# Deeper fetching of expert block rows, gating sums in four column groups, and paced weight transfers

## The chip, the cores and the metric

The kernel runs on one core of a Trainium2 chip. The metric is the device time of one execution in microseconds (us); the median of several runs is compared. A core has a matrix engine (TensorE, written PE in the profile, with its weight loads as PEld), a vector engine (VectorE, DVE), a scalar engine (ScalarE, ACT), a general engine (GpSimd, POOL) and a queue engine (SyncE, SP) that here issues most transfers. Each engine works through its own instructions in order; semaphores order them against each other and against the DMA transfers.

## The reference

Sliding-window attention with ALiBi bias, then a mixture of experts with a dense layer beside it. Shapes: q, k, v are 8 batches x 8 heads x 576 positions x 64; x has 4608 rows of 512; 8 experts, each 512 x 512 twice.

```python
scores = scale * np.matmul(q, k.transpose(0, 1, 3, 2))
mask = (rel >= 0) & (rel < 128)
scores = np.where(mask, scores + bias[None], -1000000000.0)
attn = softmax(scores)
attn_out = np.matmul(attn, v)
x = attn_out.transpose(0, 2, 1, 3).reshape(B * S, H * D)

y_dense = np.maximum(x @ w1_dense, 0.0) @ w2_dense
logits = x @ w_gate
expert_idx = np.argmax(logits, axis=1)
gate_w = softmax(logits)[np.arange(N), expert_idx]
for e in range(E):
    mask = expert_idx == e
    h = np.maximum(x[mask] @ w1[e], 0.0)
    y_moe[mask] = gate_w[mask, None] * (h @ w2[e])
return y_dense + y_moe
```

## The kernel before

**Attention.** The work is cut into 16 units (`u`): a batch and one half of its heads (four heads). A unit has three steps (`pr`): key blocks 0 and 1, 2 and 3, and the last of 64 rows; 48 steps in all. The main loop at L966 counts `n`. In round `n` it computes the scores of step `n` (`scores`, L353: a mask matmul L371, score matmuls L382, an exponential on ACT L392, and later a DVE subtraction L411 for the low half of the probabilities), multiplies the probabilities of step `n-1` with v (`attend`, L445), divides by the row sums on DVE (`norm`, L460 to L467, whose result is the tile `xf`), and transposes step `n-3` (`flip`, L488) into `xT` (fp32, for the gating) and `xTb` (bf16, for the dense layer). Rows of q, k and v of the next units are fetched by SP (`load_q` L153, `load_k` L141, `load_v` L167). `kraw` and `qraw` have one buffer each, so a fetch waits until DVE has turned the unit before (`turn`, L175). Unit 2's q is asked for twice, once ahead of the loop (L961) and once in round 1 (L1016); the second transfer follows the first.

**Gating.** When a unit's last step has been transposed, `gate_a` multiplies its half of x with its rows of `w_gate`. It runs for each half of the 576 columns: two fp32 matmuls into two 32-partition groups of a PSUM tile (L510) and one ACT copy into the tile `lt`, named `ltsb` in the profile (L517). The first half runs ahead of `attend`, the second behind it. After a batch's second unit, `gate_b` adds the groups: five fp32 matmuls with the selector `sel` (L525). An fp32 matmul is two instructions in the profile. `gate_bv`, `gate_c` and `gate_d` find the expert, the slot within the expert's rows and the gate weight, and POOL scatters the rows of x into `xs_dram` (L599). `dense1` (L647, L654) and `dense2` (L662, L670) compute the dense layer, and POOL scatters it into `ys_dram` at the same slots (L671). The small PSUM tiles of `flip`, gating and dense layer share two buffers of one tag (`misc`). The tile `yt` behind L671 has four buffers.

**Weights.** The 18 weight matrices go into `w_all` with a cast from fp32 to bf16, on POOL's queue (`load_weights`, L89). The loop sends the next one when its index is at most `2 + 16 (n-3) / 42`, which puts the first three in rounds 0, 1 and 3. From round 5 on, each is preceded by `pace` (L690): a one-element copy on POOL from `xf` into the destination, so that the transfer waits for the attention to get that far.

**Expert blocks.** Once six batches are routed, 16 blocks of 128 rows, all of one expert each, can be placed (`route_early`); the other 27 follow after the last batch (`route_late`), where SP also writes 8 pairs of fill rows behind each expert's last row (L826, L830). The blocks start in round 50, together with the last batch's dense layer, one block a round; from block 8 on they are alone. `fetch(j)` (L838) loads the block's first row into a register of SP and issues two transfers: `xr` (rows of x with gate weight and token number) and `yr` (the dense result), from four buffers each. Blocks 16 on wait for all rows and fills. `block(j)` does, in this order on PE: `turn_h(j)` (four transposes, L900, copied by ACT L904), `layer1(j+1)` (four matmuls L885, ACT L893), `turn_x(j+2)` (four transposes L864, copied by DVE L870), `layer2(j)` (four matmuls L912), then DVE adds `yr` (L920) and POOL scatters the sum to the output (L921), reading the token numbers out of `xr`. So a buffer of `xr` is free when its scatter has read it to the end. Last comes `fetch(j + AHEAD + 1)`; `AHEAD` is 3.

The order of instructions on PE, ACT and DVE is that of the program text; POOL's and SP's are set by the scheduler. SP and POOL spread their transfers over eight semaphores each, and a transfer waits until the one that had its semaphore before it is done.

Of the kernel before, what the change touches and what calls it, by code (L numbers as in the profile page):

```python
# [9 lines left out]
F32 = mybir.dt.float32  # L10
F32R = mybir.dt.float32r
BF16 = mybir.dt.bfloat16
I32 = mybir.dt.int32

ALU = mybir.AluOpType
ACT = mybir.ActivationFunctionType
AX = mybir.AxisListType
# [6 lines left out]
def kernel(  # L24
# [12 lines left out]
    nc = tc.nc  # L37

    B, H, S, D = q.shape
    E = moe_w_gate.shape[1]  # L40
    FF = moe_w1_dense.shape[1]
    DM = H * D
    NTOK = B * S
    P = 128
# [4 lines left out]
    NT = (S + P - 1) // P  # L49
    SP_ = NT * P  # L50
    HQ = H // 4
    NU = B * HQ
    R = S // 32
    PW = 2 * P
# [3 lines left out]
    NB = NTOK // P + E - 1  # L58
# [9 lines left out]
    RW = XW + 4  # L68
# [4 lines left out]
    consts = ctx.enter_context(tc.tile_pool(name="consts", bufs=1))  # L73
# [21 lines left out]
    dbuf = ph0.enter_context(tc.tile_pool(name="dbuf", bufs=1))  # L95
# [30 lines left out]
    for i in range(2):  # L126
        xrow = dbuf.tile([P, NT, RW], F32, name=f"xrow{i}")
        nc.gpsimd.memset(xrow[:, :, TC + 1 : RW], 0.0)
        xrows.append(xrow)
    lt = dbuf.tile([P, SP_], F32, name="ltsb")  # L130
    nc.gpsimd.memset(lt[:, S:SP_], 0.0)

    raw = {}
    tmp = {}
# [78 lines left out]

    mask = consts.tile([P, H, 2 * PW], BF16, name="mask")

    sc = [ppool.tile([P, 2, 2 * PW], F32, name="p32", tag=f"p32_{2 * PW}") for _ in range(2)]
    d_i, d_f = sc[0].bitcast(I32)[:, 0, :], sc[0][:, 1, :]
    inv, big = sc[1][:, 0, :], sc[1][:, 1, :]
    nc.gpsimd.iota(
# [38 lines left out]
    def more_constants():  # L258
        for h in range(4, H):
            mask_head(h)  # L260
        ut_f = ident_x["ut_f"]
        nc.vector.tensor_copy(out=ut_b, in_=ut_f)
        nc.vector.memset(ones_b, 1.0)
        nc.vector.tensor_reduce(
            out=sel,
            in_=ident_f.rearrange("p (c x) -> p x c", c=4)[:, 0:E, :],
            op=ALU.add,
            axis=AX.X,
        )
        nc.vector.tensor_single_scalar(  # L270
            out=m_div, in_=pidx_i, scalar=5, op=ALU.logical_shift_right
        )
        nc.vector.tensor_single_scalar(
            out=m_mod, in_=pidx_i, scalar=31, op=ALU.bitwise_and
        )
        nc.vector.tensor_copy(out=m_divf, in_=m_div)
        nc.vector.tensor_copy(out=m_modf, in_=m_mod)
        for i in range(NT):
            nc.vector.scalar_tensor_tensor(
                out=tok_c[:, i : i + 1],  # L280
                in0=m_modf,
                scalar=4.0 if i < NT - 1 else 2.0,
                in1=m_divf,
                op0=ALU.mult,
                op1=ALU.add,
            )
            nc.vector.tensor_scalar_add(
                out=tok_c[:, i : i + 1], in0=tok_c[:, i : i + 1], scalar1=float(i * P)
            )
        nc.vector.tensor_copy(out=em8, in_=em8_i)  # L290
        nc.vector.memset(em8[TAIL:P, NT - 1, :], 0.0)
        nc.vector.tensor_copy(out=em8x, in_=em8)
        nc.vector.memset(em8x[TAIL:P, NT - 1, :], 1.0)
        for i in range(2):
            nc.vector.memset(ohs[i][:, NT, :], 0.0)
        nc.vector.tensor_copy(out=base0, in_=base_i)
        nc.vector.tensor_copy(out=basee, in_=base_i)
        nc.vector.tensor_copy(out=jf, in_=jf_i)
        nc.vector.memset(fill_x, 0.0)
        nc.vector.tensor_copy(out=fill_x.bitcast(I32)[:, TC : TC + 1], in_=oob_f)  # L300

    ut_b = consts.tile([P, P], BF16, name="ut_b")
    ones_b = consts.tile([P, P], BF16, name="ones_b")
    sel = consts.tile([P, E], F32, name="sel")
    m_div = consts.tile([P, 1], I32, name="m_div")
    m_mod = consts.tile([P, 1], I32, name="m_mod")
    m_divf = consts.tile([P, 1], F32, name="m_divf")
# [12 lines left out]
    ident_x = {}  # L320

    def pool_constants():
        ut_f = ppool.tile([P, 2, 2 * PW], F32, name="p32", tag=f"p32_{2 * PW}")[:, 0, 0:P]
        nc.gpsimd.memset(ut_f, 1.0)
        nc.gpsimd.affine_select(
            out=ut_f,
            in_=ut_f,
            compare_op=ALU.is_gt,
            fill=0.0,
            base=0,  # L330
            pattern=[[1, P]],
            channel_multiplier=-1,
        )
        ident_x["ut_f"] = ut_f
        nc.gpsimd.memset(wg_pad, 0.0)
        nc.sync.dma_start(
            out=wg_pad[:, :, 0:E], in_=moe_w_gate.rearrange("(ds p) e -> p ds e", p=P)
        )
        nc.gpsimd.iota(em8_i, pattern=[[0, NT], [1, E]], base=-E, channel_multiplier=0)
        nc.gpsimd.iota(base_i, pattern=[[ST, E]], base=0, channel_multiplier=0)  # L340
        nc.gpsimd.iota(jf_i, pattern=[[1, NB]], base=0, channel_multiplier=0)

    wg_pad = consts.tile([P, 4, 32], F32, name="wg_pad")
    em8_i = consts.tile([P, NT, E], I32, name="em8_i")
    base_i = consts.tile([P, E], I32, name="base_i")
    jf_i = consts.tile([P, NB], I32, name="jf_i")
    pool_constants()


# [70 lines left out]
    cur = {}  # L420
# [80 lines left out]

    gst = {}

    def gate_a(u, hf):
        h0 = 64 * (u % HQ)
        HF = S // 2
        lp = psum_m.tile([P, 512], F32, name="lp", tag="misc")
        for c in range(2):
            r0 = h0 + 32 * c
            nc.tensor.matmul(  # L510
                out=lp[r0 : r0 + 32, 0:HF],
                lhsT=wg_pad[:, 2 * (u % HQ) + c, :],
                rhs=cur["xT"][:, c, hf * HF : (hf + 1) * HF],
                start=True,
                stop=True,
            )
        nc.scalar.copy(  # L517
            out=lt[h0 : h0 + 64, hf * HF : (hf + 1) * HF],
            in_=lp[h0 : h0 + 64, 0:HF],
        )  # L520

    def gate_b(b):
        gst["lg"] = lg = psum_m.tile([P, NT, E], F32, name="lg", tag="misc")
        for t in range(NT):
            nc.tensor.matmul(  # L525
                out=lg[:, t, :],
                lhsT=lt[:, t * P : (t + 1) * P],
                rhs=sel,
                start=True,
                stop=True,  # L530
            )

    def gate_bv(b):
        lg = gst["lg"]
# [86 lines left out]
    def after(nm, ins, nb):  # L621

        for b, name in writers[nm]:
            if b < nb:
# [5 lines left out]
                    ),  # L630
                    reason="rows written",
                )

    DT = [(0, 2), (2, NT)]

    def dense1(b, c, hf):
        c0, c1 = DT[hf][0] * P, min(DT[hf][1] * P, S)
# [48 lines left out]
    def pace(i):  # L686

        e, wi = divmod(i, 2)
        e = E if e == 0 else e - 1
        nc.gpsimd.tensor_copy(  # L690
            out=w_all[:TAIL, e, wi, 0, 0:1],
            in_=cur["xf"][:TAIL, 0, 0:1],
        )
# [144 lines left out]
    def fetch(j):  # L838
        r = nc.values_load(
            where[j][1],  # L840
            engines=[ENG.SP],
            min_val=0,
            max_val=NSLOT - P,
            skip_runtime_bounds_check_because="a block within an expert's rows",
        )
        xr = mpool.tile([P, RW], F32, name="xr", tag="xr", bufs=4)
        yr = mpool.tile([P, DM], F32, name="yr", tag="yr", bufs=4)
        for nm, t, src in (("x", xr, xs_dram), ("y", yr, ys_dram)):
            ins = nc.sync.dma_start(
                out=t.bitcast(I32)[:, :], in_=src[bass.DynSlice(r, P), :]  # L850
            )
            if j < NE:
                tc.declare_no_dep(
                    ins.ins, group=nm + "late", reason="rows of the first NQ batches"
                )
                tc.add_to_no_dep_group(nm + "late", ins.ins)
            after(nm, ins, NQ if j < NE else B)
        st[("r", j)] = (xr, yr)
# [74 lines left out]
        )  # L933
        tc.add_to_no_dep_group("outs", ins.ins)

    AHEAD = 3

    def block(j):
        if j == 0:
# [12 lines left out]
    with tc.manual_schedule(engines={ENG.PE, ENG.Activation, ENG.DVE}):  # L952
# [13 lines left out]
        while jm < NB:  # L966
            if 0 <= n - 3 < NS:
                flip(*steps[n - 3])
                u2, pr2 = steps[n - 3]
                b2 = u2 // HQ  # L970
                if pr2 == 2:
                    items[n] = [
                        lambda u=u2, h=h: gate_a(u, h) for h in range(2)
                    ] + items.get(n, [])
                if u2 % HQ == HQ - 1 and pr2 == 2:
                    for i, f in ((1, gate_b), (2, gate_c)):
                        items.setdefault(n + i, []).append(lambda f=f, b=b2: f(b))
                    for i, f in ((2, gate_bv), (3, gate_d)):
                        gates.setdefault(n + i, []).append(lambda f=f, b=b2: f(b))
                    for i, fs in enumerate(dense_items(b2)):  # L980
                        items.setdefault(n + 2 + i, []).extend(fs)
                    if b2 == NQ - 1:
                        gates.setdefault(n + 4, []).append(route_early)
                        gates.setdefault(n + 5, []).append(early_used)
                    if b2 == B - 1:
                        gates.setdefault(n + 5, []).append(route_late)
# [35 lines left out]
                        prep_v(u + 1)  # L1022
            if lo:
                lo()
            while wnext < 2 * (E + 1) and n < NS and wnext <= 2 + 16 * (n - 3) / 42:
                if n > 4:
                    pace(wnext)
                load_weights(wnext)
                wnext += 1
            if n == NS + 1:  # L1030
# [52 lines left out]
```

## Time and profile before

| What | us |
|---|---|
| median of 3 runs (lowest, highest) | 542.25 (536.35, 543.67) |
| profiled execution | 537.49 |
| its span, first to last instruction | 535.8 |
| PE busy, share of the span | 378.4 (71%) |
| DVE busy | 283.1 (53%) |
| ACT busy | 271.3 (51%) |
| POOL busy | 158.0 (29%) |

All durations in this document are us unless marked ns. L445 is line 445 of the kernel. "out<-in" names the tile written and the tiles read. In a list of waits, a row gives the waiting engine and line, what released it, the time waited in total, how often, and the longest. In a timeline a row gives start and duration, then engine, line and operation, and in brackets the idle time of the engine before it and its releaser; neighbouring instructions of one kind are merged (x4). Ends of matmuls are modelled, so two in a row overlap by a little.

### The profile page before, as it was taken

The numbers are of one execution on the slowest core, as the hardware profiler recorded it, in microseconds if no ns is written. First come the engines' busy times: TensorE is split into PE (matmuls) and PEld (weight loads), VectorE is DVE, ScalarE is ACT, GpSimd is POOL, SyncE is SP. The second block draws the span as 40 slices with busy tenths as digits, with TensorE's granted clock in tenths as the row PEclk, the third lists the DMA queues.
The fourth block names the chain that finished last, engine by engine and source line by source line (L and its number), as shares of the span: only waits on it lengthen the run. The fifth ranks groups of instructions, "written<-read, shape, count | busy, mean of one in ns | idle before, by whom it ended". The sixth has DMA issues, their size and how long they took to land.

```text
span 535.8 us, 11040 instructions
## 1 busy us (share of the span) xinstructions
PE 378.4 (71%) x4043; PEld 228.6 (43%) x4080; DVE 283.1 (53%) x566; ACT 271.3 (51%) x455; POOL 158.0 (29%) x193
## 2 busy tenths in 40 slices
PE   1327377898997897988988886777476557575662
PEld 0116255565555564655665453434133223232331
DVE  4736587588587676866788751225032223222221
ACT  2425076686685776876866745333233323322321
POOL 5000000534515334225246132352222222222222
PEclk9999589899999998998999999987788998989997
DMA  7842566855767884778573325346944544454450
GB/s 166 186 133 85 132 147 153 204 141 173 198 145 198 206 213 119 179 195 204 140 183 104 46 71 183 118 126 210 290 141 150 156 148 140 157 165 149 145 166 28
DMA packets 85641, 82.91 MB, mean 155 GB/s; under 512 B 43603, under 2 KB 72275, under 8 KB 85588
## 3 DMA queue, kind: packets, MB, share of 16 engines
q1 hardware_dynamic: 67512, 48.76, 32.9%
q0 software_dynamic: 17680, 33.12, 24.3%
q8 instruction: 33, 0.54, 0.4%
q10 hardware_dynamic: 396, 0.33, 0.2%
q14 instruction: 20, 0.16, 0.1%
HBM read 64.79 MB, written 28.66 MB: 174 GB/s over the span
## 4 chain that ended last, share of the span: by engine, by line
PE 30%; issue 25%; DVE 16%; ACT 8%; DMA 8%; POOL 7%; SPq 3%; POOLq 1%; another core or an unknown queue 0%; DVEq 0%; ACTq 0%
PE ax L445 7%; DVE plo L411 7%; POOL out_dram L921 7%; PE hp L647 4%; PE yp L662 4%; DMA vf<-in_v_dram 4%; PE sq L382 3%; ACT p L392 3%; PE lp L510 3%; PE sq L371 2%; DVE xf L461 2%; PE tp L488 2%; ACT qT L182 2%; SPq L167 2%; DVE qs L175 2%
## 5 line engine op out<-in xcount | busy, mean ns | idle before, releaser
L411 DVE TENSOR_TENSOR plo<-p 128x1024 bf16<-128x1024 f32 (+1 forms) x96 | 83.0, 906 | 44.8 <-ACT p L392 43.7
L445 PE MATMUL ax<-vf,p 128*128 128x65 bf16 (+1 forms) x576 | 68.5, 207 | 27.4 <-DVE xf L461 26.9
L921 POOL DMA_INDIRECT out_dram<-yo,xr x43 | 42.4, 987 | 141.8 <-DVE yo L920 123.9
L870 DVE COPY xTm<-xps 128x512 bf16<-128x512 bf16 x43 | 18.2, 424 | 123.4 <-PE xps L864 106.7
L445 PEld LDWEIGHTS <-p 128*128 128x128 bf16 (+1 forms) x1152 | 64.7, 108 | 43.8 <-DVE xf L461 31.6
L392 ACT ACTIVATE p<-sq 128x1024 f32<-128x1024 f32 (+1 forms) x96 | 69.7, 784 | 20.5 <-PE sq L382 15.0
L445 PE MATMUL ax<-vf,plo 128*128 128x65 bf16 (+1 forms) x576 | 68.2, 204 | 3.0 <-DVE plo L411 2.8
L904 ACT COPY hTm<-hps 128x512 bf16<-128x512 bf16 x43 | 25.2, 586 | 88.3 <-PE hps L900 86.7
L445 PE MATMUL ax<-vl,p 128*128 128x64 bf16 (+1 forms) x576 | 68.1, 203 | 1.3 <-DVE vl L195 0.9
L671 POOL DMA_INDIRECT ys_dram<-yt,slot x40 | 43.7, 1092 | 60.9 <-ACT yt L670 52.8
L445 PEld LDWEIGHTS <-plo 128*128 128x128 bf16 (+1 forms) x576 | 59.5, 107 | 4.5 <-DVE plo L411 4.2
L864 PE MATMUL xps<-ident_b,xr 128*128 128x128 bf16 x172 | 18.6, 236 | 54.0 <-DMA xr<-xs_dram 54.0
L599 POOL DMA_INDIRECT xs_dram<-xrow,slot x40 | 44.2, 1105 | 33.9 <-DVE xrow L591 16.4
L885 PE MATMUL hpm<-w_all,xTm 128*128 x162 | 48.5, 417 | 5.1 <-DVE xTm L870 3.6
L912 PE MATMUL y<-w_all,hTm 128*128 x167 | 47.4, 406 | 4.4 <-ACT hTm L904 3.9
L647 PE MATMUL hp<-xTb,w_all 128*128 128x256 bf16 (+1 forms) x256 | 42.1, 293 | 11.7 <-ACT hTd L654 6.9
L371 PE MATMUL sq<-mask,ident_b 128*128 128x512 bf16 (+1 forms) x183 | 39.6, 327 | 11.4 <-DVE mask L249 9.2
L893 ACT ACTIVATE hr<-hpm,xr 128x512 bf16<-128x512 f32 x43 | 29.6, 687 | 27.7 <-PE hpm L885 20.2
L864 PEld LDWEIGHTS <-xr 128*128 128x128 bf16 x172 | 12.0, 105 | 74.1 <-DMA xr<-xs_dram 70.5
L920 DVE TENSOR_TENSOR yo<-y,yr 128x512 f32<-128x512 f32 x43 | 29.7, 691 | 22.8 <-PE y L912 22.8
L662 PE MATMUL yp<-w_all,hTd 128*128 128x512 bf16 (+1 forms) x147 | 37.8, 381 | 3.6 <-issue 3.2
L654 ACT ACTIVATE hTd<-hp 128x256 bf16<-128x256 f32 (+1 forms) x64 | 26.1, 412 | 23.7 <-PE hp L647 19.8
(141 smaller groups left out, 605.9 us busy)
## 6 DMA issues: line engine op xcount, KB each, us to landing
yr<-ys_dram SPq DMA_DIRECT2D x43, 256.0 KB
kraw<-in_k_dram SPq DMA_DIRECT2D x16, 576.0 KB
qraw<-in_q_dram SPq DMA_DIRECT2D x66, 128.0 KB
vf<-in_v_dram SPq DMA_DIRECT2D x64, 128.0 KB
w_all<-in_moe_w_dram POOLq DMA_DIRECT2D x16, 512.0 KB
xr<-xs_dram SPq DMA_DIRECT2D x43, 130.0 KB
ys_dram<-fill_x SPq DMA_DIRECT2D x8, 256.0 KB
xs_dram<-fill_x SPq DMA_DIRECT2D x8, 130.0 KB
```

The lines of the kernel that those rows point to most:

```text
L371: nc.tensor.matmul(out=sq[g // 2][:, g % 2, 0:tot], lhsT=ident_b, rhs=rhs, start=True, stop=False,)
L392: nc.scalar.activation(out=p32[:, :, 0:tot], in_=sq[i][:, :, 0:tot], func=ACT.Exp, scale=SCALE,)
L411: nc.vector.tensor_tensor(out=plo[:, :, 0:tot], in0=p32[:, :, 0:tot], in1=phi[:, :, 0:tot], op=ALU.subtract,)
L445: nc.tensor.matmul(out=ax[:rows, i, o0 : o0 + w], lhsT=lhs, rhs=rhs, start=(n == 1), stop=(n == 3 * len(kl)),)
L599: ins = nc.gpsimd.indirect_dma_start(out=xs_dram[:, :], out_offset=bass.IndirectOffsetOnAxis(ap=slot[:rows, t : t + 1], axis=0), in_=xrow. ...
L647: nc.tensor.matmul(out=hp[:, 0:HF], lhsT=w_all[:, E, 0, kc, c * P : c * P + P], rhs=xTb[:, kc, c0:c1], start=(kc == 0), stop=(kc == 3),)
L662: nc.tensor.matmul(out=yp[:rows, :], lhsT=hT[:, c, t0 * P : t0 * P + rows], rhs=w_all[:, E, 1, c, :], start=(c == 0), stop=(c == 3),)
L671: ins = nc.gpsimd.indirect_dma_start(out=ys_dram[:, :], out_offset=bass.IndirectOffsetOnAxis(ap=slots[b][:rows, t : t + 1], axis=0), in_=y ...
L864: nc.tensor.transpose(out=xps[:, kc, :], in_=xr.bitcast(BF16)[:, kc * P : (kc + 1) * P], identity=ident_b,)
L885: nc.tensor.matmul(out=hp, lhsT=xT[:, kc, :], rhs=w_all[:, bass.DynSlice(er, 1), 0, kc, :], start=(kc == 0), stop=(kc == 3),)
L912: nc.tensor.matmul(out=y, lhsT=hT[:, c, :], rhs=w_all[:, bass.DynSlice(er, 1), 1, c, :], start=(c == 0), stop=(c == 3),)
L921: ins = nc.gpsimd.indirect_dma_start(out=out[:, :], out_offset=bass.IndirectOffsetOnAxis(ap=xr.bitcast(I32)[:, TC : TC + 1], axis=0), in_= ...
```

## The change

Three parts.

1. `xr` and `yr` get ten buffers instead of four, and `AHEAD` is 7 instead of 3: eight fetches are issued before the first block, and the fetch at the end of block j is that of block j+8. On SP fourteen fetches instead of eight stand ahead of the first fill row.
2. `gate_a` runs once for each unit: four fp32 matmuls into four 32-partition groups of one PSUM tile (columns 0 to 255 into the lower two, 256 to 575 into the upper two), all ahead of `attend`, then two ACT copies into a tile of the unit's own (`lts`). `gate_b` then needs two matmuls for each of the five row blocks, one a unit, with a selector that picks the lower or the upper groups.
3. The weights are sent when the index is at most `18 (n-4) / 42`, so the first three go in rounds 4, 7 and 9, and every one is preceded by `pace`.

The integer constants move into a third scratch tile, and `DT` moves up.

```diff
+    DT = [(0, 2), (2, NT)]
+    LW = S - DT[1][0] * P
+    lts = []
+    for i in range(HQ):
+        lt = dbuf.tile([P, SP_ - DT[1][0] * P], F32, name=f"lt{i}")
+        nc.gpsimd.memset(lt, 0.0)
+        lts.append(lt)
...
-    sc = [ppool.tile([P, 2, 2 * PW], F32, name="p32", tag=f"p32_{2 * PW}") for _ in range(2)]
+    sc = [ppool.tile([P, 2, 2 * PW], F32, name="p32", tag=f"p32_{2 * PW}") for _ in range(3)]
...
-        nc.vector.tensor_reduce(
-            out=sel,
-            in_=ident_f.rearrange("p (c x) -> p x c", c=4)[:, 0:E, :],
-            op=ALU.add,
-            axis=AX.X,
-        )
+        nc.vector.memset(sel, 0.0)
+        for h in range(2):
+            nc.vector.tensor_reduce(
+                out=sel[64 * h : 64 * h + 64, h, :],
+                in_=ident_f.rearrange("p (c x) -> p x c", c=4)[
+                    64 * h : 64 * h + 64, 0:E, :
+                ],
+                op=ALU.add,
+                axis=AX.X,
+            )
...
-    em8_i = consts.tile([P, NT, E], I32, name="em8_i")
-    base_i = consts.tile([P, E], I32, name="base_i")
-    jf_i = consts.tile([P, NB], I32, name="jf_i")
+    ints = sc[2].bitcast(I32)[:, 1, :]
+    em8_i = ints[:, 0 : NT * E].rearrange("p (t e) -> p t e", e=E)
+    base_i = ints[:, 64 : 64 + E]
+    jf_i = ints[:, 128 : 128 + NB]
...
-    def gate_a(u, hf):
-        h0 = 64 * (u % HQ)
-        HF = S // 2
+    def gate_a(u):
         lp = psum_m.tile([P, 512], F32, name="lp", tag="misc")
-        for c in range(2):
-            r0 = h0 + 32 * c
-            nc.tensor.matmul(
-                out=lp[r0 : r0 + 32, 0:HF],
-                lhsT=wg_pad[:, 2 * (u % HQ) + c, :],
-                rhs=cur["xT"][:, c, hf * HF : (hf + 1) * HF],
-                start=True,
-                stop=True,
-            )
-        nc.scalar.copy(
-            out=lt[h0 : h0 + 64, hf * HF : (hf + 1) * HF],
-            in_=lp[h0 : h0 + 64, 0:HF],
-        )
+        for h, (t0, t1) in enumerate(DT):
+            c0, c1 = t0 * P, min(t1 * P, S)
+            for c in range(2):
+                r0 = 64 * h + 32 * c
+                nc.tensor.matmul(
+                    out=lp[r0 : r0 + 32, 0 : c1 - c0],
+                    lhsT=wg_pad[:, 2 * (u % HQ) + c, :],
+                    rhs=cur["xT"][:, c, c0:c1],
+                    start=True,
+                    stop=True,
+                )
+        lt = lts[u % HQ]
+        nc.scalar.copy(out=lt[64:P, 0:LW], in_=lp[64:P, 0:LW])
+        nc.scalar.copy(out=lt[0:64, 0 : DT[0][1] * P], in_=lp[0:64, 0 : DT[0][1] * P])
...
         for t in range(NT):
-            nc.tensor.matmul(
-                out=lg[:, t, :],
-                lhsT=lt[:, t * P : (t + 1) * P],
-                rhs=sel,
-                start=True,
-                stop=True,
-            )
+            h = 0 if t < DT[0][1] else 1
+            c0 = (t - DT[h][0]) * P
+            for i in range(HQ):
+                nc.tensor.matmul(
+                    out=lg[:, t, :],
+                    lhsT=lts[i][:, c0 : c0 + P],
+                    rhs=sel[:, h, :],
+                    start=(i == 0),
+                    stop=(i == HQ - 1),
+                )
...
-        xr = mpool.tile([P, RW], F32, name="xr", tag="xr", bufs=4)
-        yr = mpool.tile([P, DM], F32, name="yr", tag="yr", bufs=4)
+        xr = mpool.tile([P, RW], F32, name="xr", tag="xr", bufs=10)
+        yr = mpool.tile([P, DM], F32, name="yr", tag="yr", bufs=10)
...
-    AHEAD = 3
+    AHEAD = 7
...
-                    items[n] = [
-                        lambda u=u2, h=h: gate_a(u, h) for h in range(2)
-                    ] + items.get(n, [])
+                    items[n] = [lambda u=u2: gate_a(u)] + items.get(n, [])
...
-            while wnext < 2 * (E + 1) and n < NS and wnext <= 2 + 16 * (n - 3) / 42:
-                if n > 4:
-                    pace(wnext)
+            while wnext < 2 * (E + 1) and n < NS and wnext <= 18 * (n - 4) / 42:
+                pace(wnext)
                 load_weights(wnext)
                 wnext += 1
```

More of the change, by code (lines that the diff above doesn't have):

```diff
@@ L129 @@
         xrows.append(xrow)
-    lt = dbuf.tile([P, SP_], F32, name="ltsb")
-    nc.gpsimd.memset(lt[:, S:SP_], 0.0)
+    DT = [(0, 2), (2, NT)]
[5 more added lines that the diff above has]
+        lts.append(lt)
     raw = {}
@@ L303 @@
     ones_b = consts.tile([P, P], BF16, name="ones_b")
-    sel = consts.tile([P, E], F32, name="sel")
+    sel = consts.tile([P, 2, E], F32, name="sel")
     m_div = consts.tile([P, 1], I32, name="m_div")
@@ L322, in pool_constants @@
     def pool_constants():
-        ut_f = ppool.tile([P, 2, 2 * PW], F32, name="p32", tag=f"p32_{2 * PW}")[:, 0, 0:P]
+        ut_f = sc[2][:, 0, 0:P]
         nc.gpsimd.memset(ut_f, 1.0)
@@ L632, in after @@
                 )
-    DT = [(0, 2), (2, NT)]
     def dense1(b, c, hf):
```

## The prediction

> **What bounds the kernel now.** The page comes first, for the span against which every sum is made. Then the table by stage (columns: stretch, its length, busy us of PE, weight load, DVE, ACT and POOL with instruction counts, granted TensorE clock, DMA share, GB/s).
>
> ```profile
> span 535.8 us, 11040 instructions
> ```
> ```profile
> 0.00:66.00 66.00, 23.70 (x313) 16.45 (x314) 37.65 (x78) 21.25 (x25) 7.17 (x34) 0.91 0.60 140
> 100.00:318.00 218.00, 190.16 (x2521) 123.20 (x2537) 161.76 (x313) 158.49 (x275) 83.18 (x89) 0.97 0.65 162
> 376.70:390.80 14.10, 6.13 (x29) 2.73 (x28) 1.12 (x2) 3.27 (x6) 3.80 (x4) 0.69 0.83 258
> 390.80:527.75 136.95, 88.19 (x533) 43.20 (x541) 38.23 (x68) 43.41 (x69) 34.47 (x35) 0.94 0.48 149
> ```
>
> The middle (attention with dense layers, 100 to 318) has TensorE busy 190 of 218 us: it is PE's stage. The start has no engine above 57%, and the last quarter has PE at 64% and DMA at 48%: neither is full, so each waits for something. The waits of PE (second half) and of the SP queue name it for the last quarter:
>
> ```profile
> PE xps L864 <- DMA xr<-xs_dram: 45.6, 28, 3.2
> ```
> ```profile
> SPq L849 <- DMA out_dram<-yo,xr: 111.5, 36, 9.4
> ```
>
> PE waits for a block's rows, and the queue that fetches them waits for an output scatter. The timeline shows the ring this makes:
>
> ```profile
> 444.11 0.98 POOL L921 DMA_INDIRECT out_dram<-yo,xr  x1 [4.17 <-DVE yo L920]
> ...
> 446.96 0.33 SPq L849 DMA_DIRECT2D xr<-xs_dram  x1
> ...
> 449.11 0.40 PE L864 MATMUL xps<-ident_b,xr 128*128 128x128 bf16 x4 [2.22 <-DMA xr<-xs_dram]
> ...
> 450.41 0.69 DVE L920 TENSOR_TENSOR yo<-y,yr 128x512 f32<-128x512 f32 x1 [0.44 <-PE y L912]
> ...
> 451.38 0.98 POOL L921 DMA_INDIRECT out_dram<-yo,xr  x1 [3.67 <-DVE yo L920]
> ```
>
> Block j is scattered at 444.11; its buffer is free 2.85 us later, when rows j+4 are fetched into it; 2.15 us later they are there and are transposed inside block j+2; that block's sum is scattered at 451.38. So 7.27 us for two blocks, 3.6 each; the ring of the other parity (446.73 to 455.25) gives 4.3. Over the stage it is 136.95 / 35 = 3.91 us a block. Without a wait PE needs much less:
>
> ```profile
> 441.84 0.40 PE L864 MATMUL xps<-ident_b,xr 128*128 128x128 bf16 x4 [2.45 <-DMA xr<-xs_dram]
> 442.07 1.03 PE L912 MATMUL y<-w_all,hTm 128*128 x4
> 442.94 0.39 PE L900 MATMUL hps<-ident_b,hr 128*128 128x128 bf16 x4
> ...
> 443.24 1.02 PE L885 MATMUL hpm<-w_all,xTm 128*128 x4
> ...
> 444.46 0.40 PE L864 MATMUL xps<-ident_b,xr 128*128 128x128 bf16 x4 [0.19 <-DMA xr<-xs_dram]
> ```
>
> From 441.84 to 444.46 less the wait of 0.19 is 2.43; the end of hpm (444.26) less the 0.17 by which these groups overlap the next start (442.07+1.03 against 442.94 is 0.16) gives about 2.25 at full clock.
>
> **The change part by part.** The sum is made against the profiled run's 537.49 us (span 535.8 and 1.7 around it); the median shown, 542.25, lies 4.8 above it.
>
> *Block rows, seven ahead in ten buffers.* The fetch of block k now waits for the scatter of block k-10 and is used in block k-2, so the same 7.27 us ring spans eight blocks: 0.9 us each, no bound. What is late next:
> - PE: 2.25 us at full clock. The stage's clock is 0.94. The Trainium skill ("TensorE: Matmul & The Clock Gate", HAM clock gate) says that the array is throttled only after idle windows of about 3.4 us, so without waits the clock would be full: 2.25. The row nearest, the dense middle stage, shows 0.97 while PE is 87% busy: 2.32.
> - DMA: 149 GB/s x 3.91 us is 583 KB a block. At 2.4 us that is 243 GB/s; this trace reached 258 in 376.7:390.8 and 290 in one slice of the page. It fits, closely.
> - POOL 0.98 + 0.30, ACT 0.69 + 0.59, DVE 0.42 + 0.69: below 1.3. SP: fetches that follow each other directly stand 1.6 to 1.9 us apart (384.97 to 386.56, 326.88 to 328.74). The four output buffers give 4 x 2.4 us for a scatter that lands after about 2.9.
> I take 2.5, above PE's 2.32 because DMA runs at four fifths of its time. Gain: 35 x (3.91 - 2.5) = 49 us. Ends: 2.3 (56 us) and 3.1 (28 us).
>
> *The gap before block 7.* Between the scatters of blocks 6 and 7 (376.69, 390.82) lie 14.1 us, 7.9 of them PE waiting for rows. The fetch of block 9 sits on the SP queue behind the sixteen fill writes:
>
> ```profile
> 384.97 0.39 SPq L849 DMA_DIRECT2D xr<-xs_dram  x1
> ```
>
> They start at 367.63 and end at 384.35. In the changed order fourteen fetches (blocks 0 to 13) stand ahead of the fills instead of eight; blocks 8 and 9 go to fresh buffers, and 10 to 13 wait for the scatters of blocks 0 to 3, the last at 360.6, which is before the fills can start, so the fills are not held up. Block 14, first behind the fills, is asked for at 385 and turned in block 12, at about 381.5 + 4.5 x 2.5 = 393. So block 7 leaves at about 381.5: gain 9.3. If the late fetches (block 16 on, which wait for every row and fill written) slip by over 5 us, part of this comes back.
>
> *Weights.* Three transfers of 512 KB (1 MB read each) leave the first 8 us and go to steps 4, 7 and 9. The rows that they may touch:
>
> ```profile
> 15.35 1.38 DVE L175 STREAM_TRANSPOSE qs<-qraw 128x1152 f32<-128x1152 f32 x1 [4.41 <-DMA vf<-in_v_dram]
> ...
> 36.99 1.38 DVE L175 STREAM_TRANSPOSE qs<-qraw 128x1152 f32<-128x1152 f32 x1 [9.08 <-DMA vf<-in_v_dram]
> ...
> 58.25 1.38 DVE L175 STREAM_TRANSPOSE qs<-qraw 128x1152 f32<-128x1152 f32 x1 [7.54 <-DMA vf<-in_v_dram]
> ```
>
> The wait is for q. The first 4.4 us goes (DMA share is 0.91 to 1.20 up to 20 us). The second: twelve v and k transfers took SP 10.7 us from 15.63 on; without weights I estimate 7, so 3 to 4 more. But a q load takes 6.4 to 7.6 us after its last issue even at a DMA share of 0.18 to 0.34 (41.5 to 47.9; 29.3 to 36.99), and unit 2's q is loaded twice, one after the other: that stays, and the first paced weight now falls beside it (step 2's xf, at 50.4). I give back 3 us. Net gain 5, ends -2 and 10. On POOL each costs 0.44 + 0.30 + 0.81 = 1.55 us, three 4.7 us, on an engine 29% busy; scatters queued behind a pacing copy wait for that step's xf, and who waits for them is ACT's four yt buffers and fetches after 325 us. The first dense weight is read at 91 us and the second shortly before 109 (first ys scatter); they leave at about 50 and 72. Cover gone: one weight late would cost its landing, some 7 us.
>
> *Gating.* Per unit two groups of four instructions become one group of eight; per batch the ten instructions of L525 become twenty. Rows (one unit with both halves together; one batch):
>
> ```profile
> 329.13 1.16 PE L510 MATMUL lp<-xT,wg_pad 128*32 128x288 f32 x8 [0.26 <-ACT hTd L654]
> ...
> 340.05 1.28 PE L525 MATMUL lg<-sel,ltsb 128*128 128x8 f32 x10
> ```
>
> If four column groups run at once as two do, a unit takes 0.58 x 320/288 = 0.65: 16 x 0.5 = 8 us saved. The same skill page (Part 3, what overlaps) speaks against it: weight loads overlap a running matmul only when row groups differ, and here all four share the rows; eight loads of 0.109 us and 0.53 of streaming[...] would be 1.4, a loss of 0.24 x 16 = 4. By that rule the 1.16 of today would be 1.8, so I go by the row. L525 costs 8 x 1.25 = 10 more. Net +2; ends -6 and +14; ACT copies 64x320 and 64x256 instead of twice 64x288 (0.39 each): nothing. Part lies on PE's path there; a shared PSUM slot less per unit may save some of the 5.1 us that L510 waits for L585. I book +2.
>
> *Constants.* Two memsets on POOL (0.3 more each by L118's rows) end about 4.6, before DVE needs them at 5.8; DVE's memset and second reduction are 0.3 us in the start. The integers move to a scratch tile whose last reader is at 21.87; its next writer, an exponential at 24.4, is later. Nothing.
>
> Sum: -49 -9.3 -5 +2 +0.3 = -61, so 476.5 in the profile's frame; the runs scatter by 7 us, and I name 477.
>
> **The rivals.**
> A, DMA becomes the bound of the last stage. For: 583 KB at 190 GB/s (the page's many slices of 180 to 210) is 3.07 us a block; reads and scatters share the engines. Against: 258 and 290 GB/s were reached. Gain there 29 instead of 49: 497.
> B, the ring was not the cause. The rows are late because this mix of fetch and scatter moves at 149 GB/s whatever is queued. Period 3.9; only the gap's 9 us and the start's 5 come: 525. Against: DMA share is 0.48.
> C, slower: B, and the three moved weights collide with q, which already decides steps 4 to 9: each 1 MB at 149 GB/s is 7 us on a q load that DVE waits for, 21 us, with gating's upper end +14, against -9 and -5: 558. It decides from the point where a paced weight overlaps a q load that has no slack; the trace shows such loads at 36.99 and 58.25 only, while from 73 us on the transposes start without a wait for data.
> D, the depth is not reached: each SP transfer waits for the eighth before it, so four fetches are in flight whatever the buffers. A round trip of 2.5 us over four is 0.6 us a block: no bound, unless landing takes 10 us; then 500, counted with A.
>
> **How the numbers follow.** Forecast 66% (477; its own range 460 to 490); A and D 24% (490 to 515); B 6% (520 to 540); C 4%. For 8 in 10, from 458 (period 2.3 and gating's and start's better ends in part) to 503 (most of A). Two per cent, 11 us, is about what a measurement of this kernel tells from no change: faster 0.91, same 0.05, slower 0.04.
>
> **What would show it.** PE's wait of L864 for xr falls from 45.6 us to a few; scatters of the last stage stand 2.5 us apart; DMA share there 0.7 to 0.8; no gap after block 6; L510 in groups of eight at about 0.65 us at full clock, not 1.2; the first transposition of q near 11. A period above 3 with DMA above 0.85 is A; waits of L920 for a scatter would mean the four output buffers; a stretch 0:318 that is longer than before would mean the weights or the gating cost more than I booked.

## The result, and the profile after

The changed kernel takes 490.88 us (489.69 to 492.32, 4 runs) against 542.77 us (536.35 to 543.67, 4 runs) before: ratio 0.907, 95% interval 0.901 to 0.914. It is faster by 52 us. The forecast was 477, in a range of 458 to 503. For e3 below the profile is of a slow run (543 us, where its ratio rests on the fast ones of 534 and 539), so its table shows rather more than its ratio does.

The table by stage of the changed kernel has the columns of the table before (stretch, length, busy us of PE, PEld, DVE, ACT and POOL, granted clock, DMA share, GB/s):

```profile
100.00:325.00 225.00, 192.64 (x2391) 126.79 (x2405) 151.16 (x294) 145.95 (x254) 78.81 (x85) 0.91 0.62 150
333.90:388.30 54.40, 40.33 (x235) 22.35 (x240) 16.09 (x56) 19.73 (x40) 17.49 (x18) 0.88 0.65 213
400.20:479.90 79.70, 76.16 (x515) 41.23 (x523) 37.10 (x66) 41.98 (x66) 33.24 (x34) 1.00 0.73 225
```

Two things are to be seen. The last stage is now PE's: busy 76.2 of 79.7 us at a granted clock of 1.00, with DMA at 0.73. And the middle, in which only the gating was meant to change, runs at a clock of 0.91, where it was 0.97 (100 to 318 us before).

The scatters of the last stage in the timeline (start, duration, and POOL's idle time ahead of each) stand 2.36 us apart, and L876, the new number of L864, no longer appears among PE's waits for rows there:

```profile
430.71 0.98 POOL L933 DMA_INDIRECT out_dram<-yo,xr  x1 [1.38 <-DVE yo L932]
433.06 0.98 POOL L933 DMA_INDIRECT out_dram<-yo,xr  x1 [1.38 <-DVE yo L932]
435.43 0.98 POOL L933 DMA_INDIRECT out_dram<-yo,xr  x1 [1.39 <-DVE yo L932]
```

Two cuts give the balance (us): at the third turn of q and at the first fetch of a block (325.01 before, 333.91 after).

| Stretch | before | after | difference |
|---|---|---|---|
| start to the third turn of q | 58.25 | 47.91 | -10.3 |
| from there to the first fetch | 266.76 | 286.00 | +19.2 |
| from the first fetch to the end | 210.8 | 154.0 | -56.8 |
| span | 535.8 | 487.9 | -47.9 |

The last stretch divides further: blocks 8 to 42 took 133.4 us (394.32 to 527.75) and take 79.7, a gain of 53.7; blocks 6 to 8 took 17.6 and take 11.9, a gain of 5.8; blocks 0 to 6, which run beside the last dense layers, take 41.2 instead of 38.3, a loss of 2.9.

So the fetching brought what it was forecast to bring, and the middle took 19 us back, of which 2 were booked. The experiments are about that.

### The profile page after: what moved, and what is told of

Same layout as the page of the kernel before. It is cut to its first block, busy times and chain, and to the rows that moved or that the text cites. A ratio compares the mean times of both kernels' runs of the same rounds, so it can differ in the third digit from the quotient of the medians.

```text
span 487.9 us, 11194 instructions
## 1 busy us (share of the span) xinstructions
PE 388.2 (80%) x4123; PEld 242.4 (50%) x4160; DVE 284.3 (58%) x568; ACT 271.9 (56%) x455; POOL 159.5 (33%) x197
## 4 chain that ended last, share of the span: by engine, by line
PE 38%; issue 19%; DVE 12%; POOL 11%; ACT 10%; DMA 6%; SPq 1%; POOLq 1%; another core or an unknown queue 1%; ACTq 0%; DVEq 0%
PE ax L457 9%; POOL out_dram L933 8%; PE yp L674 6%; DMA qraw<-in_q_dram 5%; PE sq L394 4%; PE sq L383 4%; PE lg L539 4%; PE hp L659 4%; DVE plo L423 4%; ACT kT L191 3%; PE lp L522 3%; PE tp L500 2%; ACT p L404 2%; ACT qT L188 2%; DVE xf L473 2%
## 5 line engine op out<-in xcount | busy, mean ns | idle before, releaser
L457 PEld LDWEIGHTS <-p 128*128 128x128 bf16 (+1 forms) x1152 | 65.9, 109 | 34.4 <-DVE xf L473 16.5
L457 PE MATMUL ax<-vf,p 128*128 128x65 bf16 (+1 forms) x576 | 69.8, 208 | 14.3 <-DVE xf L473 13.7
L457 PE MATMUL ax<-vf,plo 128*128 128x65 bf16 (+1 forms) x576 | 68.9, 205 | 4.2 <-DVE plo L423 2.8
L457 PE MATMUL ax<-vl,p 128*128 128x64 bf16 (+1 forms) x576 | 69.3, 204 | 2.5 <-issue 1.4
L683 POOL DMA_INDIRECT ys_dram<-yt,slot x40 | 44.7, 1118 | 61.2 <-ACT yt L682 53.7
L457 PEld LDWEIGHTS <-plo 128*128 128x128 bf16 (+1 forms) x576 | 60.3, 108 | 5.6 <-DVE plo L423 4.4
L882 DVE COPY xTm<-xps 128x512 bf16<-128x512 bf16 x43 | 18.2, 424 | 67.7 <-PE xps L876 31.0
L383 PE MATMUL sq<-mask,ident_b 128*128 128x512 bf16 (+1 forms) x183 | 46.0, 365 | 12.3 <-DVE mask L255 9.0
L897 PE MATMUL hpm<-w_all,xTm 128*128 x162 | 45.1, 394 | 9.4 <-DVE xTm L882 4.0
L924 PE MATMUL y<-w_all,hTm 128*128 x167 | 46.1, 398 | 4.1 <-issue 3.0
L659 PE MATMUL hp<-xTb,w_all 128*128 128x256 bf16 (+1 forms) x256 | 40.3, 290 | 5.7 <-ACT hTd L666 4.9
L674 PE MATMUL yp<-w_all,hTd 128*128 128x512 bf16 (+1 forms) x147 | 39.4, 393 | 2.1 <-issue 2.0
L507 ACT COPY xT<-tp 128x512 f32<-128x512 f32 (+1 forms) x48 | 23.1, 480 | 30.7 <-PE tp L500 28.4
L500 PE MATMUL tp<-ident_f,xf 128*128 128x128 f32 (+1 forms) x160 | 27.8, 290 | 14.9 <-ACT yt L682 5.6
```

Source lines behind the costliest of these rows:

```text
L383: nc.tensor.matmul(out=sq[g // 2][:, g % 2, 0:tot], lhsT=ident_b, rhs=rhs, start=True, stop=False,)
L457: nc.tensor.matmul(out=ax[:rows, i, o0 : o0 + w], lhsT=lhs, rhs=rhs, start=(n == 1), stop=(n == 3 * len(kl)),)
L500: nc.tensor.transpose(out=tp[:, i, c, 0:rows], in_=xf[:rows, i, c * P : c * P + P], identity=ident_f[:rows, :rows],)
L659: nc.tensor.matmul(out=hp[:, 0:HF], lhsT=w_all[:, E, 0, kc, c * P : c * P + P], rhs=xTb[:, kc, c0:c1], start=(kc == 0), stop=(kc == 3),)
L674: nc.tensor.matmul(out=yp[:rows, :], lhsT=hT[:, c, t0 * P : t0 * P + rows], rhs=w_all[:, E, 1, c, :], start=(c == 0), stop=(c == 3),)
L683: ins = nc.gpsimd.indirect_dma_start(out=ys_dram[:, :], out_offset=bass.IndirectOffsetOnAxis(ap=slots[b][:rows, t : t + 1], axis=0), in_=y ...
```

## The experiments

The kernel before was measured anew beside each group of experiments: 524.0 us beside e1 to e4, 519.5 beside e5 to e8, 542.4 beside e9 to e11. Why its level differs is not known; the first and the last group ran on the same chip. So times in us are compared only within a group, and ratios to the kernel before across groups. Such ratios carry over only roughly: the changed kernel has 0.907 in the first measurement and 0.884 in e5.

**One part at a time.** e1 has only the deeper fetching:

```diff
-        xr = mpool.tile([P, RW], F32, name="xr", tag="xr", bufs=4)
-        yr = mpool.tile([P, DM], F32, name="yr", tag="yr", bufs=4)
+        xr = mpool.tile([P, RW], F32, name="xr", tag="xr", bufs=10)
+        yr = mpool.tile([P, DM], F32, name="yr", tag="yr", bufs=10)
...
-    AHEAD = 3
+    AHEAD = 7
```

> The kernel before with ten buffers and AHEAD 7 alone. From the first fetch to the end the changed kernel takes 154.0 us against 210.8 before. If that stretch is all the fetching's, this kernel gives 542.8 - 57 = 486, with the stretch up to the first fetch (325.0 before) unchanged. If part of it came from the other two edits (more steady clock, other buffer places), 495 or more.

454.0 us, ratio 0.870 (0.864 to 0.876). Better than expected, and better than the whole change (0.907, or 0.884 in e5): a part of the change seems to cost time. From the first fetch to the end it takes 141.5 us (311.49 to 453.0).

e2 has only the weights' new times:

```diff
-            while wnext < 2 * (E + 1) and n < NS and wnext <= 2 + 16 * (n - 3) / 42:
-                if n > 4:
-                    pace(wnext)
+            while wnext < 2 * (E + 1) and n < NS and wnext <= 18 * (n - 4) / 42:
+                pace(wnext)
```

> The kernel before with the later, paced weights alone. Theory G (gating makes the middle longer): only the start gains, 10 us as in the changed kernel's third turn of q (58.25 to 47.91), so 532. Theory W (the weight transfers moved into the steps make the middle 19 us longer): 542.8 - 10 + 19 = 552.

515.0 us, ratio 0.984 (0.980 to 0.988): a gain of 8.5 us, and no sign of theory W.

e3 has only the gating (the changed kernel with the two edits above undone):

> The kernel before with the new gating alone. Theory G: the 19 us by which the middle got longer are here, so 562, batch periods of 41 us instead of 37, granted clock in the middle 0.92 instead of 0.97. Theory W: 545, periods of 37.

540.9 us, ratio 1.028 (1.018 to 1.039): 15 us slower (0.028 x 524). Theory G.

e4 is the reverse, the changed kernel with the gating of before:

> The changed kernel with the gating of before (deep fetching and late weights stay). Theory G: 490.9 - 19 = 472 and batch periods of 37 us. Theory W: 491, periods of 41.

448.1 us, ratio 0.859 (0.851 to 0.867). The two tables show the middle of e3 and of e4, each stretch about a batch long, from a scatter of one batch's rows to one of the next; columns as above. First e3, then e4:

```profile
210.90:247.04 36.14, 32.74 (x412) 21.63 (x411) 25.73 (x45) 25.98 (x44) 13.81 (x15) 0.91 0.71 169
247.04:283.30 36.26, 33.07 (x403) 21.53 (x401) 25.37 (x45) 25.66 (x44) 12.22 (x15) 0.91 0.72 179
```
```profile
194.48:226.68 32.20, 29.61 (x400) 19.23 (x399) 24.94 (x44) 25.57 (x44) 15.19 (x16) 0.95 0.82 201
226.68:259.26 32.58, 29.98 (x392) 18.99 (x389) 25.42 (x45) 26.14 (x45) 13.17 (x14) 0.97 0.82 197
```

About 4 us more a batch with the new gating, PE busy 3 us longer, the clock at 0.91 instead of 0.96. The level of 37 and 41 us that was expected belongs to the first measurement; the difference is about the same here.

**What in the gating costs.** The timeline of the changed kernel shows a candidate. First PE, then ACT, at a unit's last step:

```profile
219.48 0.63 PE L522 MATMUL lp<-xT,wg_pad 128*32 128x256 f32 x4
221.42 1.28 PE L522 MATMUL lp<-xT,wg_pad 128*32 128x320 f32 x4 [1.31 <-ACT xT L507]
```
```profile
219.01 2.19 ACT L191 CAST kT<-ks 128x1152 fp32r<-128x1152 f32 x1
221.09 0.28 ACT L507 COPY xT<-tp 128x128 f32<-128x128 f32 x1
```

The second pair of gating matmuls needs columns 512 to 575, which ACT copies in this very step, behind a copy of 2.19 us for k. Before the change the pair that read these columns stood behind `attend`, and the 48 matmuls there covered the copy. Now PE waits 1.31 us with `attend` queued behind the pair. Over the whole run such waits come to 9.9 us, where L510 in the kernel before had none for `xT`:

```profile
PE lp L522 <- ACT xT L507: 9.9, 10, 1.3
```

The six longest, of 1.25 to 1.33 us, come at the first unit of six of the batches. The table of the place above shows what follows there:

```profile
220.30:221.40 1.10, 0.00 (x0) 0.00 (x0) 1.07 (x3) 1.10 (x3) 0.44 (x1) 0.98 0.24 63
221.40:222.60 1.20, 1.18 (x4) 0.19 (x4) 1.20 (x2) 0.48 (x3) 0.83 (x1) 0.50 0.29 100
222.60:224.00 1.40, 1.40 (x28) 1.37 (x27) 0.33 (x2) 0.79 (x2) 0.00 (x0) 0.50 0.95 185
```

The clock falls to 0.50 for the pair and for most of `attend`. The four groups are torn apart too: 0.63 and 1.28 here, 0.62 and 0.73 where the clock stays full (99.55), instead of one group. e5 is the changed kernel in the group of e6 to e8, and e6 moves the gating behind `attend`:

```diff
-                    items[n] = [lambda u=u2: gate_a(u)] + items.get(n, [])
+                    items[n] = [lambda: None, lambda u=u2: gate_a(u)] + items.get(n, [])
```

> The changed kernel itself, on the chip of the next three runs, so that they can be compared with it. Ratio to the kernel before 0.907 as measured; if the parts add up as the first four runs have them (ratio 0.859 with the gating of before, and 0.028 for gating alone), 0.887.

> The changed kernel with gate_a behind attend instead of ahead of it. Theory X (ahead of attend, the second pair of L522 waits for the last xT copy of ACT, PE stands idle for 1.3 us and its clock falls for the multiplications that follow): that wait is covered by attend, and the time falls by 6 to 15 us, ratio 0.015 to 0.03 lower, clock of the middle back to 0.95 or more. Theory L (the cost is the ten further instructions of L539 a batch, 8 x 1.25 = 10 us): no change.

e5: 461.3 us, ratio 0.884 (0.875 to 0.893), where the parts of the first four runs add up to 0.887. e6: 449.9 us, ratio 0.867 (0.860 to 0.873): 11.4 us less. The stretch from 120 to 280 us, first of e5, then of e6:

```profile
120.00:280.00 160.00, 144.04 (x1854) 97.11 (x1864) 116.36 (x225) 114.86 (x199) 65.60 (x70) 0.93 0.70 174
```
```profile
120.00:280.00 160.00, 139.82 (x1985) 96.29 (x1994) 129.28 (x254) 120.81 (x211) 77.46 (x76) 0.98 0.72 182
```

In the same time e6 does more instructions on every engine, with PE less busy: its clock is 0.98 instead of 0.93. And the gating is one group of eight:

```profile
170.97 0.74 PE L522 MATMUL lp<-xT,wg_pad 128*32 128x256 f32 x8
```

The pause itself is not what e6 saves. PE's waits for `xT` ahead of L522 are gone (10.2 us in e5), but PE waits as much longer for `xf` ahead of `attend`, e5 first:

```profile
PE ax L457 <- DVE xf L473: 17.0, 7, 6.3
```
```profile
PE ax L457 <- DVE xf L473: 28.3, 12, 7.9
```

What falls is PE's busy time, for as many instructions, e5 first:

```profile
PE 378.8 (82%) x4123; PEld 241.6 (52%) x4160; DVE 284.3 (62%) x568; ACT 271.3 (59%) x455; POOL 160.6 (35%) x197
```
```profile
PE 360.6 (81%) x4123; PEld 232.6 (52%) x4160; DVE 283.3 (63%) x568; ACT 269.2 (60%) x455; POOL 167.5 (38%) x197
```

That is 18.2 us, where the span falls by 14.1. L522 itself has 8.6 of it (22.0 to 13.5: its groups are no longer torn), and L457 6.5 (75.6 to 69.2, at the higher clock).

e7 keeps that place and has ACT move the halves into one `lt`, so that L539 is ten instructions a batch again:

```diff
+        h0 = 64 * (u % HQ)
+        cm = DT[1][0] * P
-        nc.scalar.copy(out=lt[64:P, 0:LW], in_=lp[64:P, 0:LW])
-        nc.scalar.copy(out=lt[0:64, 0 : DT[0][1] * P], in_=lp[0:64, 0 : DT[0][1] * P])
+        nc.scalar.copy(out=lt[h0 : h0 + 64, cm : cm + LW], in_=lp[64:P, 0:LW])
+        nc.scalar.copy(out=lt[h0 : h0 + 64, 0:cm], in_=lp[0:64, 0:cm])
...
```

> As e6, but the two ACT copies bring both column halves into one lt tile in the layout of the kernel before (a copy may move partitions), so that L539 is five matmuls again. Theory L: 10 us less than e6, ratio 0.02 lower. If four column groups at once save 0.5 us a unit over two groups, this is below the kernel with the gating of before by 8 us; if they do not overlap, equal to it (0.859).

439.5 us, ratio 0.849 (0.841 to 0.857): 10.4 us less than e6. Theories X and L both hold, each for its part. The two rows that L is about, e6 first:

```profile
179.37 2.40 PE L539 MATMUL lg<-sel,lt 128*128 128x8 f32 x20
```
```profile
175.64 1.28 PE L530 MATMUL lg<-sel,ltsb 128*128 128x8 f32 x10
```

1.12 us a batch by these rows is 9 of the 10.4. The group L522 itself (0.74 against two of 0.68 in the kernel before) saves 0.6 a unit, 10 us over sixteen. Against e4, e7 is 0.010 lower in ratio, 5 us, but the intervals of the two overlap, so that the time alone does not show this saving; the row does. The intervals of e6 and e7 in one group are apart.

**The start.** e8 is e4 without the first of unit 2's two q loads:

```diff
         load_v(1)
-        load_q(2, nc.sync)
```

> The kernel of e4 (deep fetching, late weights, gating of before) without the first of the two loads of unit 2's q. If that doubled load is what DVE waits for at the third turn of q (5 to 6 us), the time is 5 us lower than e4's ratio of 0.859 gives, 0.85. If q is late for another reason (the paced weight beside it), equal to e4.

438.1 us, ratio 0.845 (0.837 to 0.852); e4, of another group, has 0.859 (0.851 to 0.867), so that by the ratios alone the gain is not certain. The turn of unit 2's q, first in e4 and then in e8 (in brackets: DVE's wait for the load):

```profile
50.38 1.38 DVE L175 STREAM_TRANSPOSE qs<-qraw 128x1152 f32<-128x1152 f32 x1 [6.05 <-DMA qraw<-in_q_dram]
```
```profile
42.44 1.38 DVE L175 STREAM_TRANSPOSE qs<-qraw 128x1152 f32<-128x1152 f32 x1
```

The wait is gone and the turn 7.9 us earlier: the doubled load was the cause. In e8 the paced weight is sent at 42.88, just after the turn, so e8 does not tell what it costs beside a q load. Two traces do: with it (sent at 44.70 in e4) the wait is 6.05, and in the kernel before, which sends no weight between 6.63 and 67.35, it was 7.54.

**All together.** e9 is e7 with this edit:

> The kernel of e7 (gating behind attend, one lt tile) and unit 2's q loaded once, as in e8. If the two gains are separate, e7's ratio 0.849 less the 0.014 that the single load brought: 0.835. If the start's gain is taken back by a later wait, 0.845 to 0.849.

452.3 us, ratio 0.836 (0.821 to 0.851), the lowest of all and what the sum of the two gains gives. But its interval holds e7 and e8 as well, so that the two gains add is not shown. Against the changed kernel's 0.907, or 0.884, it is clearly faster.

**The ring.** e10 and e11 are the changed kernel with fewer buffers:

```diff
-        xr = mpool.tile([P, RW], F32, name="xr", tag="xr", bufs=10)
-        yr = mpool.tile([P, DM], F32, name="yr", tag="yr", bufs=10)
+        xr = mpool.tile([P, RW], F32, name="xr", tag="xr", bufs=6)
+        yr = mpool.tile([P, DM], F32, name="yr", tag="yr", bufs=6)
...
-    AHEAD = 7
+    AHEAD = 5
```

(e11: 5 and 4.)

> The changed kernel with six buffers and AHEAD 5. By the ring (7.3 to 8.5 us over two blocks with four buffers, here over four blocks: 1.8 to 2.1) PE's 2.36 us a block stays the bound in the last stage; only the gap before block 7 may return in part, since two fetches fewer stand ahead of the fills. If the depth itself matters (eight fetches under way against DMA congestion), the period is above 2.5.

> The changed kernel with five buffers and AHEAD 4. The ring goes over three blocks: 7.3 / 3 = 2.4 to 8.5 / 3 = 2.8 us a block, so a period of 2.4 to 2.8 with PE waiting for rows again in part of the blocks. If the ring reading is wrong and only the time at which fetches start counts, 3.5 or more.

Single runs, so only the traces' spacings count: from block 8 to block 42, 34 blocks.

| Buffers | us a block | PE's wait for rows, from 300 us on | blocks 6 to 8 |
|---|---|---|---|
| 4 (before) | 3.92 | 54.0, of them 7.9 ahead of block 7 | 17.6 |
| 5 (e11) | 3.00 | 17.2 | 14.1 |
| 6 (e10) | 2.51 | 2.3 | 8.9 |
| 10 (changed) | 2.34 | none listed | 11.9 |

PE's waits in e11 and in e10, from 300 us on (total, times, longest):

```profile
PE xps L876 <- DMA xr<-xs_dram: 17.2, 16, 3.9
```
```profile
PE xps L876 <- DMA xr<-xs_dram: 2.3, 4, 1.0
```

The ring is confirmed: one more buffer gives 0.9 us a block, two more come within 0.17 us of ten. Five are at 3.0, above the 2.4 to 2.8 that the ring of before gives, six at 2.5, above PE's 2.36; why the ring is somewhat longer when it runs faster was not tried. The part of the e10 expectation that the gap before block 7 would come back did not show.

## Why the prediction was right, point by point

- *Block rows.* The step was right. PE became the bound, busy 2.24 us a block (76.2 over 34 blocks; 2.25 was read off); the stage's clock is 1.00, as the rule that the prediction takes from the skill page has it, and not the 0.97 of the row nearest. 2.34 us a block against 2.5 booked: 53.7 us over these 34 blocks instead of 49 over 35. DMA carries 225 GB/s at a share of 0.73: rival A did not come. Rivals B and D fall with the period.
- *The gap before block 7.* It shrank, by 5.8 us over two blocks rather than the 9.3 booked. PE has no wait for rows there any more, but 7.4 us remain between the scatters of blocks 6 and 7 (388.34 and 395.77), with 3.6 us of the last dense layer's matmuls in them (L674 at 387.12); the prediction had block 7 leave 4.8 us after block 6. Blocks 0 to 6 lost 2.9 (38.3 to 41.2). The gating is the likely cause: e9, which has the deep fetching with the gating of e7, in a group in which the kernel before has the same level, has 38.2. Its parts were not tried apart there.
- *Weights.* A gain of 5 booked, with ends of -2 and 10; measured 8.5 (e2). The giving back of 3 us for a paced weight beside the doubled q load did not happen: that wait is not longer with the weight beside it (6.05 in e4) than without (7.54 before), and what makes the load late is its doubling (e8). Rival C, which had such collisions cost 21 us, did not come.
- *Gating.* Here the prediction failed. It booked +2, with ends of -6 and +14; the middle grew by 19.2, and e3 finds +15 in the whole time. L539's ten further instructions were right in size (10 booked; 10.4 from e6 to e7). The four column groups were read rightly where they run as one: 0.5 us a unit booked, 0.6 in e6 (0.74 against two of 0.68), and not the loss that the prediction works out from the skill page's rule on weight loads (with 0.53 us of streaming, an estimate that no row here shows). But in the changed kernel they do not run as one, and the 8 us booked came as 2: all instructions of the line are busy for 22.7 us, where it was 24.8 before and is 13.5 in e6. The step that failed is the move, which is no term of the sum. The text counts two groups of four that become one of eight, and does not ask what the second group stood behind. It goes from behind `attend` to ahead of it, where ACT's copy of the last 64 columns is not covered: 11.4 us (e5 to e6), most of it as torn groups and a lower clock, not as the pause.
- *Constants.* Nothing was booked, and they were not tried alone. The first turn of q comes at 11.5, near the 11 that was forecast.

The sum: 477 was forecast in the profile's frame as 476.5, and the profiled run took 489.7. Of the 13 between them, the middle is 17, the start -5, the last part (first fetch to the end) about 1.5. That the measured time lies within the range is partly luck: the range's upper end was made from rival A, which did not come, and the gating took that place.

## What to carry to other kernels

A transfer into a buffer that waits for another transfer out of it makes a ring; divide its length by the blocks that lie between, and compare it with the engine's own time a block: here six buffers came within about 7% of ten, and four cost 67% more a block. When an instruction is moved ahead of another on an in-order engine, ask for each of its operands who writes it in this step, and which work covered that until now; packing two halves together moves one of them. And when a layout saves instructions at one end, count those that it adds where the parts are summed: a copy that is made anyway could put them in the old order.

## What the runs showed of the hardware

A pause of 1.3 us on PE was followed by the clock at 0.50 for 2.6 us and more (220.3 to 224, in the table of that place). That is shorter than the idle windows of about 3.4 us that the prediction takes from the skill page as the only cause of throttling; where they differ, the trace decides. But a pause of 1.32 us, between the same instructions of an earlier batch in the same execution, left the clock at 1.00:

```profile
98.30:99.50 1.20, 0.00 (x0) 0.00 (x0) 1.17 (x3) 1.20 (x3) 0.91 (x2) 1.00 0.56 213
99.50:100.30 0.80, 0.76 (x7) 0.24 (x8) 0.80 (x1) 0.50 (x3) 0.79 (x1) 1.00 0.95 327
100.30:102.00 1.70, 1.70 (x50) 1.63 (x51) 0.74 (x4) 0.79 (x2) 0.05 (x1) 1.00 0.78 151
```

In e6 a pause of 1.10 us ahead of `attend` left it at 1.00 too:

```profile
168.40:169.60 1.20, 0.23 (x7) 0.23 (x8) 1.13 (x4) 1.20 (x1) 0.93 (x2) 1.00 0.26 92
169.60:171.00 1.40, 1.40 (x51) 1.35 (x48) 1.40 (x2) 1.02 (x5) 1.09 (x2) 1.00 0.56 209
```

Of the six waits above 1.2 us, five were followed by the pair at 1.16 to 1.28 us instead of 0.73; in e5, the same program, two of six. So such a short pause can be enough, and isn't always. The narrow fp32 matmuls ahead of it (32 columns each) do not decide it alone, since they are the same in every case; what does is open.

The same program took about 542 us on two occasions and 520 to 524 on two others, and the cause is not known. The one program profiled at both levels is the changed kernel, with spans of 487.9 and 460.3 us (e5): of these 27.6 us, 14 lie between the first scatters of x of the second and of the seventh batch (120.39 to 325.81; 121.86 to 313.00 in e5), and 15 behind; up to there e5 is 1.5 later. In e5 the clock was 0.93 on the mean, against 0.92.
